# Splitting the PSUM ring, moving tables and casts, and halving the last chunk in a state-space and windowed-attention kernel

## The chip, the cores and the metric

The kernel runs on one core of one Trainium2 chip. The metric is the device time of one execution in microseconds (us), median of several. A profiled execution of each kernel gives the trace; its span is about 2 us shorter than its time. In tables and text, PE is TensorE's matmuls, DVE is VectorE, ACT is ScalarE, POOL is GpSimd and SP is the engine that issues most transfers. PSUM is the memory into which TensorE's matmuls write in these kernels, and SBUF is the one that holds tables and inputs; a *ring* is a pool of equal buffers that are taken in turn.

## The reference, cut to what matters

Four layers, each with a residual: a state-space convolution, a windowed attention, the same convolution again with the same parameters, and the attention again. The input has 2048 positions and 512 channels, in bf16.

```python
def _A_ref(u, A_re, A_im, B_re, B_im, C_re, C_im, log_dt, Dskip):
    ...
    P = jnp.exp(logdA[:, :, None] * l[None, None, :])           # 512 x 128 x 2048 powers
    K = jnp.einsum("dn,dnl,dn->dl", Cc, P, dB).real             # kernel: 512 x 2048
    ...                                                         # y = irfft(rfft(u) * rfft(K)) + u * Dskip
def _B_ref(x, wqkv, wo):      # H = 32 heads of 16, window W = 8, dilation 2
    ...
x = x + _A_ref(_layernorm(x), ...)      # first convolution: makes K too
x = x + _B_ref(_layernorm(x), ...)      # attention 1
x = x + _A_ref(_layernorm(x), ...)      # second convolution: K's spectra are reused
x = x + _B_ref(_layernorm(x), ...)      # attention 2
```

## The kernel before

The kernel `K` is not made by 2048 powers. A *ladder* squares the complex multipliers, VectorE builds two small *tables* of powers (`Xtab`, `Ytab`/`Y2tab`) per half chunk of 64 channels by repeated doubling, and TensorE contracts them (`psk`). There are eight such tables.

The convolution works on four chunks of 128 channels. `s1` is the first FFT stage (matmuls with a constant, copied out as `Z`). `s2` transposes `Z` (copied out as `zt`) and does the second stage; the spectra are `xc` for the input and `Kt` for the kernel. `finish` multiplies them (`pa`, `pb`, on VectorE), does the inverse of the second stage (`VT`) and the output stage, which adds the residual into `X`.

```python
def s2(self, Z, dst, what):
    for ch in range(2):
        pt = self.pst([128, 2, 2, 4, 128], BF)          # same PSUM ring as everything else
        ...                                             # 16 transposes
        zt = self.w.tile([128, 2, 2, 512], BF, name="zt", tag="zt")
        self.evac("zt", ...)                            # one copy of 128x2048
        for c2 in range(2):
            xp = self.pst([128, 2, 512])
            ...                                         # four matmuls
            self.evac(what, dst[:, ch * 2 + c2, :, :], xp[:])

def kernel_and_first_conv(...):
    ...
    ladder(nc, pp, pst, identf, raw, MA, MB, cb, nu, fill)
    # the ladder's SBUF is given back here; the tables are laid in it afterwards
    psum = es.enter_context(tc.tile_pool(name="k_ps", bufs=4, space=PSUM))
    T = Tables(nc, tc, es, MA, MB, cb, nu, psum, kscr)  # psk comes from the ring too
    cv = Conv(nc, tc, es, C, X, psum, ())               # every copy on ScalarE
    ...
    for dc in range(4):
        ...                                             # two tables, u_fft(dc), k_fft(dc-1), finish(dc-1)
    Kt = k_fft(3)
    cv.finish(3, xcs.pop(3), Kt)

def a_layer(...):                                       # second convolution
    ...
    for g in range(NG):
        ln_stats_group(...)                             # statistics, with TensorE idle
    for dc in range(4):
        xc = cv.u_fft(dc, rstd, nb, "dve")
        cv.finish(dc, xc, Kts[dc])
```

Of the kernel before, what the change touches and what calls it, by code (L numbers as in the profile page):

```python
# [72 lines left out]
def make_consts(nc, const, C):  # L73
    fc = _fft_consts()
    bones_np = np.zeros((128, 8), dtype=np.float32)
    for f in range(128):
        bones_np[f, f // 16] = 1.0
    for name in ("F1", "F1T"):
        C[name + "_h"] = nc.inline_tensor(_bf(fc[name]), name="c_" + name)
    todo = [("ident", _bf(np.eye(128)), BF), ("C2", _bf(fc["C2"]), BF), ("IC", _bf(fc["IC"]), BF),  # L80
            ("bones", _bf(bones_np), BF), ("onesr", _bf(np.ones((1, 128))), BF)]
    for i, (name, arr, dt) in enumerate(todo):
        h = nc.inline_tensor(arr, name="c_" + name)
        t = const.tile(list(arr.shape), dt, name="sb_" + name)
        (nc.sync if i % 2 == 0 else nc.scalar).dma_start(t[:], h.ap())
        C[name] = t


def load_f1(nc, pool, C):
    for name, eng in (("F1", nc.sync), ("F1T", nc.scalar)):  # L90
# [4 lines left out]
def load_x(nc, const, x2d):  # L95
    xv = x2d.rearrange("(p j) d -> p j d", j=NJ)
    X = const.tile([128, NJ, D], BF, name="X")
    for g in range(NG):
        (nc.sync if g % 2 == 0 else nc.scalar).dma_start(X[:, g * 4:(g + 1) * 4, :], xv[:, g * 4:(g + 1) * 4, :])
# [30 lines left out]
def ln_stats_group(nc, small, Xt, rstd, nb):  # L130
    stats = small.tile([128, 4, 6], F32, name="ln_stats", tag="ln_stats")
    mv = small.tile([128, 4, 2], F32, name="ln_mv", tag="ln_mv")
    for jj in range(4):
        nc.vector.bn_stats(stats[:, jj, :], Xt[:, jj, :])  # L134
    for jj in range(4):
        nc.vector.bn_aggr(mv[:, jj, :], stats[:, jj, :])
    mvb = small.tile([128, 4, 2], BF, name="ln_mvb", tag="ln_mvb")
    nc.vector.tensor_copy(mvb[:], mv[:])
    veps = small.tile([128, 4], BF, name="ln_veps", tag="ln_veps")
    nc.vector.tensor_scalar(veps[:], mvb[:, :, 1], EPS, None, ALU.add)  # L140
    den = small.tile([128, 4], BF, name="ln_den", tag="ln_den")
    nc.scalar.activation(den[:], veps[:], ACT.Sqrt)
    nc.vector.reciprocal(rstd, den[:])
    nc.vector.scalar_tensor_tensor(nb, mvb[:, :, 0], -1.0, rstd, ALU.mult, ALU.mult)


def layer_norm_group(nc, small, Xt, out_ap):
    rstd = small.tile([128, 4], F32, name="ln_rstd", tag="ln_rstd")
    nb = small.tile([128, 4], F32, name="ln_nb", tag="ln_nb")
    ln_stats_group(nc, small, Xt, rstd[:], nb[:])  # L150
    for jj in range(4):
        nc.vector.tensor_scalar(out_ap[:, jj, :], Xt[:, jj, :], rstd[:, jj:jj + 1], nb[:, jj:jj + 1],
                                ALU.mult, ALU.add)


class Conv:


    def __init__(self, nc, tc, es, C, X, psum, on_dve, zbufs=2, pbufs=2):
        self.nc, self.C, self.X, self.ps, self.on_dve = nc, C, X, psum, on_dve  # L160
# [5 lines left out]
    def pst(self, shape, dt=F32):  # L166
        return self.ps.tile(shape, dt, name="ps", tag="ps")
# [7 lines left out]
    def s1(self, rhs_j, drow=None):  # L175
        nc, F1 = self.nc, self.C["F1"]
        Z = self.z.tile([128, 2, 16, 128], BF, name="Z", tag="Z")
        for jq in range(NJ // 4):
            ps = self.pst([128, 2, 16, 32])
            for jj in range(4):  # L180
                j = jq * 4 + jj
                for r in range(2):
                    dk = drow is not None and j == 0 and r == 0
                    o = ps[:, r, :, jj * 8:(jj + 1) * 8]
# [3 lines left out]
            self.evac("z", Z[:, :, :, jq * 32:(jq + 1) * 32], ps[:])  # L188
        return Z

    def s2(self, Z, dst, what):
        nc, ident, C2 = self.nc, self.C["ident"], self.C["C2"]
        for ch in range(2):
            pt = self.pst([128, 2, 2, 4, 128], BF)
            for c2 in range(2):
                for r in range(2):
                    for g in range(4):
                        nc.tensor.transpose(pt[:, c2, r, g, :], Z[:, r, (ch * 2 + c2) * 4 + g, :], ident[:])  # L198
            zt = self.w.tile([128, 2, 2, 512], BF, name="zt", tag="zt")
            self.evac("zt", zt[:].rearrange("q c r k -> q (c r k)"), pt[:].rearrange("q c r g k -> q (c r g k)"))  # L200
            for c2 in range(2):
                xp = self.pst([128, 2, 512])
                nc.tensor.matmul(xp[:, 0, :], C2[:, 0, :], zt[:, c2, 0, :], start=True, stop=False)  # L203
                nc.tensor.matmul(xp[:, 0, :], C2[:, 2, :], zt[:, c2, 1, :], start=False, stop=True)
                nc.tensor.matmul(xp[:, 1, :], C2[:, 1, :], zt[:, c2, 0, :], start=True, stop=False)  # L205
                nc.tensor.matmul(xp[:, 1, :], C2[:, 0, :], zt[:, c2, 1, :], start=False, stop=True)  # L206
                self.evac(what, dst[:, ch * 2 + c2, :, :], xp[:])

    def u_fft(self, dc, rstd, nb, norm_eng):
        nc = self.nc  # L210
        dsl = slice(dc * DCH, (dc + 1) * DCH)
        U = self.one.tile([128, NJ, DCH], BF, name="U", tag="U")
        for j in range(NJ):
            if norm_eng == "act":
                nc.scalar.activation(U[:, j, :], self.X[:, j, dsl], ACT.Identity, bias=nb[:, j:j + 1],
                                     scale=rstd[:, j:j + 1])
            else:
                nc.vector.tensor_scalar(U[:, j, :], self.X[:, j, dsl], rstd[:, j:j + 1], nb[:, j:j + 1],
                                        ALU.mult, ALU.add)
        Z = self.s1(lambda j: U[:, j, :])  # L220
        xc = self.one.tile([128, 4, 2, 512], BF, name="xc", tag="xc", bufs=2)
        self.s2(Z, xc, "xc")
        return xc

    def finish(self, dc, xc, Kt):
        nc, IC, F1T, X = self.nc, self.C["IC"], self.C["F1T"], self.X
        dsl = slice(dc * DCH, (dc + 1) * DCH)
        VT = self.one.tile([128, 2, NJ, DCH], BF, name="VT", tag="VT")

        def inverse(c, pa, pb):  # L230
# [8 lines left out]
            for gh in range(2):  # L239
                self.evac("vt%d" % gh,  # L240
                          VT[:, :, :, c * 32 + gh * 16:c * 32 + gh * 16 + 16].rearrange("k r j x -> k (r j) x"),
# [3 lines left out]
        for c in range(5):  # L245
            cur = None
            if c < 4:
# [8 lines left out]
        for jh in range(2):  # L256
            ps = self.pst([128, 2, 4, DCH])
            for q in range(2):
                j0 = jh * 8 + q * 4
                nc.tensor.matmul(ps[:, q, :, :], self.C["ident"][:], X[:, j0:j0 + 4, dsl], start=True, stop=False,  # L260
                                 skip_group_check=True)
                for jj in range(4):
                    for r in range(2):
                        nc.tensor.matmul(ps[:, q, jj, :], F1T[:, j0 + jj, r, :], VT[:, r, j0 + jj, :],
                                         start=False, stop=(jj == 3 and r == 1), skip_group_check=True)
            nc.scalar.copy(X[:, jh * 8:(jh + 1) * 8, dsl], ps[:].rearrange("p q j d -> p (q j) d"))


def load_params(nc, pp, prm):
    raw = {}  # L270
    engs = [nc.sync, nc.scalar]
# [4 lines left out]
    for idx, name in enumerate(("A_im", "A_re", "C_re", "B_re", "C_im", "B_im")):  # L276
        t = pp.tile([128, 4, NM], BF, name="raw_" + name)
        engs[(idx + 1) % 2].dma_start(t[:], prm[name].rearrange("(t p) n -> p t n", p=128))
# [4 lines left out]
def ladder(nc, pp, pst, identf, raw, MA, MB, cb, nu, fill):  # L283
# [4 lines left out]
    nc.vector.tensor_copy(dtf[:], dtb[:])  # L288
    dt_bc = dtf[:].unsqueeze(2).to_broadcast([128, 4, NM])
# [4 lines left out]
    nc.vector.tensor_tensor(tb[:], raw["A_im"][:], dt_bc, ALU.mult)  # L294
    a = tmp("a_arg")
    nc.vector.tensor_tensor(a[:], raw["A_re"][:], dt_bc, ALU.mult)
    e = tmp("e_mag")
    nc.scalar.activation(e[:], a[:], ACT.Exp)
    nc.vector.tensor_scalar(tb[:], tb[:], 1.0 / TWO_PI, None, ALU.mult)
# [3 lines left out]
    nc.vector.tensor_tensor(ws[:], tb[:], rnd[:], ALU.subtract)  # L303
    sn = tmp("sn")
    nc.scalar.activation(sn[:], ws[:], ACT.Sin, scale=TWO_PI)
    tq = tmp("tq")
    rnd2 = tmp("rnd2")
    wc = tmp("wc")
    nc.vector.tensor_scalar(tq[:], tb[:], 0.25, None, ALU.add)
    nc.vector.tensor_scalar(rnd2[:], tq[:], MAGIC, MAGIC, ALU.add, ALU.subtract)  # L310
    nc.vector.tensor_tensor(wc[:], tq[:], rnd2[:], ALU.subtract)
    cs = tmp("cs")
    nc.scalar.activation(cs[:], wc[:], ACT.Sin, scale=TWO_PI)
    quad = pp.tile([128, 4, 4, NM], F32, name="quad")
    nc.vector.tensor_tensor(quad[:, :, 1, :], e[:], sn[:], ALU.mult)
    nc.vector.tensor_tensor(quad[:, :, 0, :], e[:], cs[:], ALU.mult)
# [30 lines left out]
    def multipliers(i, cur):  # L347
# [8 lines left out]
        nc.vector.tensor_scalar(MB[:, i, :, 0, :], src[:, 1], -1.0 if conj else 1.0, None, ALU.mult)  # L356
        nc.vector.tensor_scalar(MB[:, i, :, 1, :], src[:, 1], 1.0 if conj else -1.0, None, ALU.mult)
# [29 lines left out]
class Tables:  # L387
# [59 lines left out]
    def contract(self, X, Y, Y2, hc):  # L447

        nc = self.nc
        psk = self.ps.tile([128, 16, EY], F32, name="psk", tag="ps")  # L450
# [20 lines left out]
def kernel_and_first_conv(nc, tc, C, prm, X, raw_pool, kt_dram, kscr):  # L471
    with ExitStack() as es:
# [5 lines left out]
        rstd = mt.tile([128, NJ], F32, name="rstd")  # L478
        nb = mt.tile([128, NJ], F32, name="nb")
        small = es.enter_context(tc.tile_pool(name="k_small", bufs=2))  # L480
        with tc.tile_pool(name="k_prep", bufs=1) as pp, tc.tile_pool(name="k_pst", bufs=2, space=PSUM) as pst:
            raw = load_params(nc, pp, prm)
            identf = pp.tile([128, 128], F32, name="identf")
            nc.scalar.dma_start(identf[:], nc.inline_tensor(np.eye(128, dtype=np.float32), name="c_identf").ap())
            X = load_x(nc, raw_pool, X)
            make_consts(nc, raw_pool, C)
            load_f1(nc, mt, C)
# [3 lines left out]
            def fill(i):  # L491
                if 1 <= i <= 4:
                    g = i - 1
                    ln_stats_group(nc, small, X[:, g * 4:(g + 1) * 4, :], rstd[:, g * 4:(g + 1) * 4],
                                   nb[:, g * 4:(g + 1) * 4])
# [312 lines left out]
```

## Time and profile before

Median 750.1 us (749.71 to 750.54). The span of the profiled run is 746.9 us. Its stages, with borders read from the trace at the first and last instruction of a kind:

| border | us |
|---|---|
| first contraction (first `psk` matmul) | 75.4 |
| last table finished (last `Y2tab`) | 268.2 |
| last output of the first convolution (`X`) | 309.7 |
| attention 1: first transpose (`pt_x`) | 321.2 |
| second convolution: first `s1` matmul | 483.4 |
| its last `X` | 586.4 |
| attention 2: first transpose | 591.4 |
| end | 746.9 |

The next fence shows busy time by stretch of the kernel before: the stretch in us, its length, busy us and instructions of PE, PEld (weight loads), DVE, ACT and POOL, then the mean granted TensorE clock (1.00 is full), the DMA share and GB/s.

```profile
0.00:75.40 75.40, 18.68 (x95) 11.16 (x96) 64.00 (x149) 57.23 (x83) 0.60 (x8) 0.98 0.21 72
75.40:268.20 192.80, 118.03 (x2570) 85.83 (x2580) 151.91 (x268) 106.75 (x129) 1.69 (x12) 0.77 0.11 37
268.20:309.70 41.50, 26.04 (x432) 19.49 (x432) 6.22 (x10) 18.87 (x21) 0.96 (x1) 0.75 0.10 39
309.70:321.20 11.50, 0.00 (x0) 0.00 (x0) 9.23 (x24) 0.20 (x1) 5.10 (x1) 0.61 0.62 183
483.40:586.40 103.00, 79.22 (x716) 59.82 (x720) 56.24 (x126) 48.74 (x58) 0.00 (x0) 0.87 0.05 20
```

No engine is full over the whole span, but VectorE dominates the first two stretches (64 of 75 us, then 152 of 193), and TensorE dominates the second convolution (79 of 103). So in each stage the question is what the dominant engine waits for. The waits of VectorE between 100 and 270 us (engine and tile that waited, the releaser, us in total, times, longest):

```profile
DVE Ytab L433 <- PE psk L461: 21.5, 3, 7.2
DVE pa L250 <- ACT Kt L173: 15.4, 6, 6.9
```

At every other table VectorE stands up to 7.2 us until the contraction has finished reading an older one, and then for the kernel's spectrum. The waits of TensorE in the second convolution (484 to 591 us):

```profile
PE ps L203 <- DVE zt L171: 10.6, 8, 1.4
PE ps L198 <- ACT Z L173: 8.7, 4, 2.5
PE ps L264 <- DVE VT L171: 2.5, 4, 1.0
```

TensorE loses 2.7 us a chunk before the second-stage matmuls, because they wait for the transposed copy `zt`, and 2.2 us before the transposes, because they wait for `Z`. These three waits, 21.8 us, are nearly all of the 23.8 us in which PE is idle there.

### The profile page before, as it was taken

To read this page: it belongs to the slowest core of one execution; us is meant where nothing else is said; L and a number is where in the kernel's file an instruction comes from. 1 tells how busy PE (TensorE), PEld (TensorE's weight loads), DVE (VectorE), ACT (ScalarE), POOL (GpSimd) and SP (SyncE) were. 2 spreads that over 40 slices of the span, in tenths; PEclk is the share of its full clock that TensorE was granted. 3 is DMA by queue.
4 is the path that set the end of the run, shared out by engine and by line. 5 is a ranking of instruction groups with operands and counts; after the bars stand their busy time and mean duration, and the time that the engine had idled before them with its cause. 6 is when DMAs were issued, how large, how long until landed. Compare 5 with 4: busy or idle time off the path is not lost.

```text
span 746.9 us, 13529 instructions
## 1 busy us (share of the span) xinstructions
PE 479.3 (64%) x5863; PEld 304.3 (41%) x5908; DVE 506.0 (68%) x936; ACT 363.3 (49%) x436; POOL 8.4 (1%) x21
## 2 busy tenths in 40 slices
PE   0215166756756747459971889376787589934996
PEld 0212144543643534444551344155665445631443
DVE  4999996598598531482698983775544724998870
ACT  2998058468556526346433144344544365512434
POOL 0000000000000000300000000000000000000000
PEclk9999656887887885859985899779998789955999
DMA  8000000210200200500030000710000000030011
GB/s 288 0 0 1 29 31 1 86 31 1 86 31 1 86 31 1 169 1 0 2 101 0 1 0 1 279 59 1 2 1 1 0 1 1 2 99 0 1 57 56
DMA packets 14682, 28.75 MB, mean 38 GB/s; under 512 B 4769, under 2 KB 10274, under 8 KB 12834
## 3 DMA queue, kind: packets, MB, share of 16 engines
q1 hardware_dynamic: 10640, 20.26, 8.1%
q10 hardware_dynamic: 3984, 7.64, 2.8%
q8 instruction: 46, 0.75, 0.4%
q14 instruction: 12, 0.10, 0.0%
HBM read 15.86 MB, written 8.39 MB: 32 GB/s over the span
## 4 chain that ended last, share of the span: by engine, by line
PE 45%; DVE 29%; ACT 15%; issue 8%; DMA 3%; ACTq 0%; DVEq 0%
PE ps_qk L599 8%; PE po L710 5%; PE ps_o L727 4%; ACT Z L173 4%; PE ps_v L612 4%; ACT zt L173 4%; PE ps L198 3%; DVE ln_stats L134 3%; PE ps L203 2%; DVE Ytab L442 2%; DVE prodpv L704 2%; PE ps L205 2%; PE ps L206 2%; PE Lp L642 2%; DVE Y2tab L444 2%
## 5 line engine op out<-in xcount | busy, mean ns | idle before, releaser
L710 PE MATMUL po<-prodpv,sb_ident 128*128 128x512 bf16 x248 | 67.0, 402 | 35.0 <-DVE prodpv L696 31.3
L599 PE MATMUL ps_qk<-xnT,wqk 128*128 128x512 bf16 x248 | 59.7, 392 | 8.3 <-ACT xnT L586 7.4
L134 DVE BATCH_NORM_STATS2 ln_stats<-X 128x6 f32<-128x512 bf16 x64 | 43.0, 709 | 30.5 <-PE ps_o L727 12.3
L250 DVE TENSOR_TENSOR pa<-xc,Kt 128x1024 bf16<-128x1024 bf16 x32 | 22.0, 689 | 53.4 <-ACT Kt L173 38.5
L173 ACT CAST Z<-ps 128x1024 bf16<-128x1024 f32 x48 | 45.8, 1025 | 25.0 <-PE ps L185 25.0
L198 PE MATMUL ps<-sb_ident,Z 128*128 128x128 bf16 x384 | 35.4, 265 | 33.4 <-ACT Z L173 33.4
L710 PEld LDWEIGHTS <-sb_ident 128*128 128x128 bf16 x256 | 26.1, 102 | 67.1 <-issue 45.7
L696 DVE TENSOR_TENSOR prodpv<-V,Lsb 128x2048 bf16<-128x2048 bf16 (+1 forms) x40 | 42.2, 1115 | 16.3 <-PE po L710 16.0
L203 PE MATMUL ps<-zt,sb_C_99 128*128 128x512 bf16 x48 | 25.2, 525 | 43.0 <-ACT zt L173 32.4
L173 ACT CAST xc<-ps 128x1024 bf16<-128x1024 f32 x32 | 31.9, 1013 | 41.7 <-PE ps L206 41.7
L198 PEld LDWEIGHTS <-Z 128*128 128x128 bf16 x384 | 32.0, 123 | 42.0 <-ACT Z L173 35.9
L642 PE MATMUL Lp<-sb_bones,prodqk 128*128 128x8 bf16 x1024 | 34.5, 167 | 12.7 <-DVE prodqk L638 7.2
L173 ACT CAST VT<-ps 128x512 bf16<-128x512 f32 x48 | 26.5, 587 | 30.5 <-PE ps L238 30.5
L599 PEld LDWEIGHTS <-wqk 128*128 128x128 bf16 x256 | 25.6, 100 | 38.5 <-issue 11.8
L642 PEld LDWEIGHTS <-prodqk 128*128 128x128 bf16 x1024 | 32.2, 98 | 21.8 <-DVE prodqk L638 8.7
L458 PE MATMUL psk<-Ytab,Xtab 128*32 128x64 bf16 x1024 | 22.6, 208 | 26.7 <-DVE Ytab L442 18.0
L727 PE MATMUL ps_o<-wo_t,oT 128*128 128x512 bf16 x124 | 32.3, 379 | 6.7 <-ACT o L713 4.3
L236 PE MATMUL ps<-sb_IC,pb 128*128 128x256 bf16 x128 | 35.2, 275 | 1.0 <-DVE pb L251 1.0
L235 PE MATMUL ps<-sb_IC,pa 128*128 128x256 bf16 x128 | 35.3, 276 | 0.7 <-DVE pa L250 0.7
L237 PE MATMUL ps<-sb_IC,pb 128*128 128x256 bf16 x128 | 35.1, 274 | 0.0
L238 PE MATMUL ps<-sb_IC,pa 128*128 128x256 bf16 x128 | 35.0, 274 | 0.0
L173 ACT COPY zt<-ps 128x2048 bf16<-128x2048 bf16 x16 | 29.8, 1865 | 7.6 <-PE ps L198 7.4
(176 smaller groups left out, 1134.0 us busy)
## 6 DMA issues: line engine op xcount, KB each, us to landing
kt_scratch<-Kt SPq DMA_DIRECT2D x4, 1024.0 KB, 4.1
Vp<-V SPq DMA_DIRECT2D x2, 1568.0 KB, 9.6
sb_F1T<-c_F1T ACTq DMA_DIRECT2D x2, 1024.0 KB, 6.8
k_scratch<-KTq SPq DMA_DIRECT2D x8, 256.0 KB, 2.0
KT<-k_scratch SPq DMA_DIRECT2D x8, 256.0 KB, 2.8
Kt<-kt_scratch SPq DMA_DIRECT2D x2, 1024.0 KB, 14.6
Kt<-kt_scratch ACTq DMA_DIRECT2D x2, 1024.0 KB, 17.0
X<-in_A_u_dram ACTq DMA_DIRECT2D x2, 512.0 KB
```

The source lines that it names most:

```text
L134: nc.vector.bn_stats(stats[:, jj, :], Xt[:, jj, :])
L173: self.nc.scalar.copy(dst, src)
L198: nc.tensor.transpose(pt[:, c2, r, g, :], Z[:, r, (ch * 2 + c2) * 4 + g, :], ident[:])
L203: nc.tensor.matmul(xp[:, 0, :], C2[:, 0, :], zt[:, c2, 0, :], start=True, stop=False)
L235: nc.tensor.matmul(o, pa[:, 0, sl], IC[:, 0, :], start=True, stop=False)
L236: nc.tensor.matmul(o, pb[:, 1, sl], IC[:, 1, :], start=False, stop=False)
L237: nc.tensor.matmul(o, pb[:, 0, sl], IC[:, 2, :], start=False, stop=False)
L599: nc.tensor.matmul(ps[:, sc * 512:(sc + 1) * 512], wqk[:, ct, which * 512 + ft * 128: which * 512 + (ft + 1) * 128], xnT[:, ct, s0:s0 + 51 ...
L642: nc.tensor.matmul(Lp[f2][:, w, jj, :], pr[:, f2, jj * 128:(jj + 1) * 128], bones[:], start=True, stop=True)
L696: nc.vector.tensor_tensor(p2[:, ja - j0: ja - j0 + n, :].rearrange("p j (t d h) -> p (j t) d h", t=4, d=DH), V[:, ja - sh: ja - sh + n, :] ...
L710: nc.tensor.matmul(po[jj // 2][:, jj % 2, :], ident[:], p2[:, jj, :], start=(w == 0), stop=(w == W - 1))
L727: nc.tensor.matmul(ps[:, jj, :], oT[:, ft, j * 128:(j + 1) * 128], wo_t[:, ft, :], start=(ft == 0), stop=False)
```

## The change

The intent: give contraction, spectra and transposes PSUM buffers of their own; lay the tables where the ladder's memory isn't, so that they can begin before it is finished; take the casts of the multipliers off VectorE; and do the last chunk of the first convolution in two halves. The diff does more: it moves the layer norm statistics into the stage before, moves the first convolution's 64 normalizations and its input `zt` copies from ScalarE to VectorE, makes every `zt` copy half as large, gives `VT` a second buffer in the second convolution, and issues the second convolution's next transform ahead of this chunk's inverse. Cut to its core:

```diff
@@ ladder
-        nc.vector.tensor_scalar(MB[:, i, :, 0, :], src[:, 1], -1.0 if conj else 1.0, None, ALU.mult)
+        nc.scalar.activation(MB[:, i, :, 0, :], src[:, 1], ACT.Copy, scale=-1.0 if conj else 1.0)
         ...                                                    # and MB[..., 1, :]
@@ kernel_and_first_conv
+        psk = es.enter_context(tc.tile_pool(name="k_psk", bufs=1, space=PSUM))
+        T = Tables(nc, tc, es, MA, MB, cb, nu, psk, kscr)      # before the ladder's pools
         with tc.tile_pool(name="k_prep", bufs=1) as pp, ...:
             ...
-        psum = es.enter_context(tc.tile_pool(name="k_ps", bufs=4, space=PSUM))
-        T = Tables(nc, tc, es, MA, MB, cb, nu, psum, kscr)
-        cv = Conv(nc, tc, es, C, X, psum, ())
+        psT = es.enter_context(tc.tile_pool(name="k_psT", bufs=2, space=PSUM))
+        psA = es.enter_context(tc.tile_pool(name="k_psA", bufs=2, space=PSUM))
+        cv = Conv(nc, tc, es, C, X, psA, psT, ("zt_xc",))      # the input's zt on VectorE
         ...
-        Kt = k_fft(3)
-        cv.finish(3, xcs.pop(3), Kt)
+        ln_b.gather(X, 0, 0, NJ)                               # statistics of three chunks of X
+        xc = xcs.pop(3)
+        for h in range(2):
+            Kt = k_fft(3, h, h + 1)
+            cv.finish(3, xc, Kt, h * 2, h * 2 + 2)
+        ln_b.gather(X, 1, 0, NJ)
+        ln_b.finish(0, NJ)
@@ u_fft
-            if norm_eng == "act":
-                nc.scalar.activation(U[:, j, :], self.X[:, j, dsl], ACT.Identity, bias=..., scale=...)
-            else: ...
+            ln.norm(U[:, j, :], self.X[:, j, dsl], j)          # tensor_scalar on VectorE
@@ a_layer (second convolution)
+        xcs = {0: cv.u_fft(0, ln)}
         for dc in range(4):
-            xc = cv.u_fft(dc, rstd, nb, "dve")
-            cv.finish(dc, xc, Kts[dc])
+            if dc < 3:
+                xcs[dc + 1] = cv.u_fft(dc + 1, ln)
+            cv.finish(dc, xcs.pop(dc), Kts[dc])
+            if dc == 2:
+                ln_b.gather(X, 0, 0, NJ)
+        ln_b.gather(X, 1, 0, NJ)
+        ln_b.finish(0, NJ)
@@ ... (load queues, one range reduction less in the ladder, product buffers of attention 4 -> 3)
```

## The prediction

> **What bounds the kernel now.** Stages, from the timeline: first convolution with kernel generation (0 to 309 us), attention (to 472), second convolution (to 586), attention. From busy time by stretch and the waits:
> - Prologue: ladder starts at 26.5 us, first table whole at 75.3; VectorE has 64 us of work there.
> - Generation (100 to 270): VectorE busy 128 of 170 us; it waits 21.5 us for the contraction (psk) and 15.4 for Kt. One ring of four serves all PSUM users, so it stands behind FFT evictions. The Trainium skill (Perfetto Trace Analysis, Optimization Strategy) names such consistent bubbles as a sign of too little PSUM; the trace agrees (7.2 us at each odd table).
> - Tail (273 to 309): a serial chain, VectorE idle 22.7 us, then 12 us of weights and layer norm before attention's first transpose at 321.2.
> - Second convolution: 25 us a chunk, PE busy 19 to 20, waiting for Z (8.7 us in all) and zt (10.6). Before it, 10.4 us of layer norm with PE idle.
>
> **What the change does, costed.**
> 1. Prologue: 22 multiplier casts (0.34 us of VectorE each) go to ScalarE, one range reduction goes, ScalarE issues three loads instead of nine. VectorE work falls by 9 us and starts at 4.5 us instead of 10: first table at about 63 us. ScalarE (2.9 us a level) ends near 50.
> 2. Generation: own PSUM for the contraction removes most of both waits, but 64 normalizations (0.23 us) and 16 half-size zt copies (0.63) come onto VectorE: 24 us. From 63: seven tables of 20.2, plus 13.7, 10.1, 14.4 for spectrum products, 4 of stalls: last table at 247 instead of 268. Gain of 1 and 2 together: 21.
> 3. Tail: the order of instructions puts the halves one after the other on PE and ScalarE, and the weight reorder before the second half's products on VectorE: about 40 us instead of 37. Statistics and weights come earlier: attention starts 6 us after the last X instead of 11.5. Gain 2.
> 4. Attention: normalization no longer waits for statistics, 3 us each, twice. Three product buffers instead of four and statistics in the value stage lose 2.
> 5. Second convolution: statistics ride in the attention before: gain 7.5. The next chunk's transform ahead of this one's inverse, and finer zt: about 21.5 us a chunk, gain 14.
>
> Sum: 21 + 2 + 6 - 2 + 7.5 + 14 = 48.5. Predicted 702 us, range 684 to 722. Chances: faster 0.95, same 0.04, slower 0.01.
>
> The 128x512 spectra matmul takes 0.63 us after a gap and 0.38 in a dense stretch. The Trainium skill (TensorE: Matmul & The Clock Gate, Part 1) says activity releases the throttle; fewer gaps should raise the clock in the second convolution above 0.87.
>
> **What shows it.** First contraction at 60 to 66 us; from there VectorE over 92% busy to the last table at 243 to 253; its waits for psk and Kt under 8 us together; last table to attention's first transpose 50 to 53 us; attention's end to the next first-stage matmul about 3 us; chunk period of the second convolution 20 to 23 us; PE's wait for zt there under 5 us.
>
> **What would make it wrong.** VectorE, in program order, stalling for zt or U (a generation chunk over 54 us); PE waiting for PSUM with two wide buffers; a tail over 45 us; the second convolution staying at 25.

## The result, and the profile after

The changed kernel takes 695.25 us (693.33 to 697.3, 4 runs) against 750.14 us (4 runs) of the kernel before on the same chip. The ratio is 0.9269, 95% interval 0.9241 to 0.9296. Ratios here are the mean time of one kernel's fast runs over that of the other's of the same rounds, so not quite the ratio of the quoted medians. It is faster, inside the predicted range and 7 us below its centre.

The same view for the kernel after, by its own stage borders:

```profile
0.00:61.90 61.90, 5.51 (x22) 3.40 (x22) 54.74 (x117) 41.73 (x60) 0.61 (x8) 1.00 0.26 87
61.90:238.30 176.40, 123.74 (x2652) 90.76 (x2661) 168.69 (x346) 90.11 (x105) 1.51 (x12) 0.87 0.11 41
238.30:279.90 41.60, 26.04 (x498) 18.93 (x496) 15.65 (x34) 20.51 (x30) 6.06 (x1) 0.84 0.28 90
279.90:285.40 5.50, 0.02 (x1) 0.03 (x2) 4.98 (x36) 0.21 (x1) 0.00 (x0) 0.68 0.00 0
435.10:536.10 101.00, 79.55 (x716) 59.53 (x720) 62.67 (x149) 48.15 (x56) 0.00 (x0) 0.90 0.08 31
```

Set against the fence of before, line by line: the prologue is 13.5 us shorter; the table stage is 16.4 us shorter although VectorE does 16.8 us more work in it (it is now busy 168.69 of 176.40 us, 95.6%); the tail has the same length; the gap before attention is halved; and the second convolution, where the largest single gain of a later stage was expected, is 2 us shorter. All stages, from the two traces:

| stage | before, us | after, us | change | predicted |
|---|---|---|---|---|
| to first contraction | 75.4 | 61.9 | -13.5 | about -12 |
| first contraction to last table | 192.8 | 176.4 | -16.4 | about -9 |
| last table to last `X` | 41.5 | 41.6 | +0.1 | about +3 |
| last `X` to attention 1 | 11.5 | 5.5 | -6.0 | about -5 |
| attention 1, to its last `X` | 151.8 | 146.6 | -5.2 | -2 |
| layer norm before the second convolution | 10.4 | 3.1 | -7.3 | -7.5 |
| second convolution | 103.0 | 101.0 | -2.0 | -14 |
| last `X` to attention 2 | 5.0 | 5.1 | +0.1 | 0 |
| attention 2 | 155.5 | 150.2 | -5.3 | -2 |
| sum | 746.9 | 691.4 | -55.5 | -48.5 |

The first two rows were predicted as one term, 21; the split follows from the 63 us that the prediction gave for the first table. The next two were one term too (gain 2), and the attention's 6 less 2 is put half on each.

The waits of VectorE after, 60 to 260 us:

```profile
DVE pa L262 <- ACT Kt L180: 5.9, 1, 5.9
DVE zt L178 <- PE pt L208: 5.0, 7, 1.3
```

The wait for `psk`, 21.5 us before, is gone. The one wait for `Kt` is that of the last chunk, after the last table. And the waits of TensorE in the second convolution, 438 to 535 us:

```profile
PE pt L208 <- ACT Z L180: 7.7, 4, 2.1
PE psA L276 <- DVE VT L178: 5.5, 4, 1.4
PE psA L247 <- DVE pa L262: 4.0, 1, 4.0
PE psA L219 <- DVE zt L178: 0.9, 2, 0.7
```

This is where the expected 14 us went. The wait for `zt` did fall as predicted, from 10.6 to 0.9 us. But the wait for `VT` rose from 2.5 to 5.5, a new wait of 4.0 for `pa` appeared, and the one for `Z` stayed. So 9.7 us were gained on one wait, and 7.0 lost on one that grew and one that is new. What VectorE does in the last chunk shows one of them (VectorE's instructions in order: start, us, what, count, and the idle time before it):

```profile
515.15 0.68 DVE L178 CAST VT<-psA 128x512 bf16<-128x512 f32 x1
518.24 7.46 DVE L146 BATCH_NORM_STATS2 ln_st_b<-X 128x6 f32<-128x384 bf16 x16 [2.40 <-ACT X L278]
525.61 1.27 DVE L178 CAST VT<-psA 128x512 bf16<-128x512 f32 x2
526.80 0.68 DVE L262 TENSOR_TENSOR pa<-xc,Kt 128x1024 bf16<-128x1024 bf16 x1
```

Sixteen statistics for the next layer norm stand in VectorE's queue before the last chunk's copies. VectorE runs its queue in order, so the copies wait behind 7.46 us of work that nothing needs yet. The Trainium skill (PSUM — Partial Sum Buffer, section Engine vs sequencer instructions) says that these queues are strict FIFO; this trace agrees. In the steady chunks a smaller form of the same thing happens: the products of chunk c+1 stand before the copy of chunk c. When `X` is written out by ScalarE shows the period:

```profile
470.28 2.12 ACT L278 CAST X<-psA 128x1024 bf16<-128x1024 f32 x2 [2.79 <-PE psA L276]
493.67 2.12 ACT L278 CAST X<-psA 128x1024 bf16<-128x1024 f32 x2 [2.72 <-PE psA L276]
517.19 2.12 ACT L278 CAST X<-psA 128x1024 bf16<-128x1024 f32 x2 [2.72 <-PE psA L276]
```

A chunk takes 23.4 us, with PE busy for some 19 of them.

### The profile page after: what moved, and what is told of

It reads as the page before. It is cut to its first block, busy times and chain, and to the rows that moved or that the text cites. A ratio compares the mean times of both kernels' runs of the same rounds, so it can differ in the third digit from the quotient of the medians.

```text
span 691.4 us, 13674 instructions
## 1 busy us (share of the span) xinstructions
PE 465.4 (67%) x5930; PEld 297.7 (43%) x5977; DVE 512.5 (74%) x984; ACT 331.3 (48%) x388; POOL 8.2 (1%) x21
## 5 line engine op out<-in xcount | busy, mean ns | idle before, releaser
L193 PE MATMUL psA<-U,sb_F_128 128*128 128x128 bf16 x256 | 24.1, 242 | 47.5 <-issue 38.5
L180 ACT CAST Z<-psA 128x1024 bf16<-128x1024 f32 (+1 forms) x52 | 46.4, 960 | 20.1 <-issue 17.3
L180 ACT CAST xc<-psA 128x1024 bf16<-128x1024 f32 x32 | 32.0, 1012 | 44.6 <-PE psA L222 37.4
L193 PEld LDWEIGHTS <-sb_F_128 128*128 128x128 bf16 x416 | 27.1, 104 | 57.9 <-issue 50.7
L208 PE MATMUL pt<-sb_ident,Z 128*128 128x128 bf16 x384 | 38.4, 268 | 19.5 <-ACT Z L180 19.5
L180 ACT CAST VT<-psA 128x512 bf16<-128x512 f32 x48 | 26.6, 588 | 44.4 <-PE psA L250 44.4
L660 PE MATMUL Lp<-sb_bones,prodqk 128*128 128x8 bf16 x1024 | 35.3, 167 | 14.7 <-DVE prodqk L656 9.4
L247 PE MATMUL psA<-sb_IC,pa 128*128 128x256 bf16 x128 | 36.2, 283 | 9.6 <-DVE pa L262 9.6
L159 DVE TENSOR_SCALAR U<-X,ln_rstd_a,ln_nb_a 128x128 bf16<-128x128 bf16 x128 | 33.5, 307 | 7.2 <-PE psA L193 7.2
L178 DVE COPY zt<-pt 128x1024 bf16<-128x1024 bf16 x32 | 21.8, 688 | 20.6 <-PE pt L208 20.5
L248 PE MATMUL psA<-sb_IC,pb 128*128 128x256 bf16 x128 | 36.2, 283 | 1.1 <-DVE pb L263 1.1
L249 PE MATMUL psA<-sb_IC,pb 128*128 128x256 bf16 x128 | 36.0, 281 | 0.0
L250 PE MATMUL psA<-sb_IC,pa 128*128 128x256 bf16 x128 | 35.9, 281 | 0.0
```

Source lines behind the costliest of these rows:

```text
L180: self.nc.scalar.copy(dst, src)
L193: nc.tensor.matmul(o, F1[:, j, r, :], rhs_j(j), start=True, stop=not dk)
L208: nc.tensor.transpose(pt[:, r, g, :], Z[:, r, i * 4 + g, :], ident[:])
L247: nc.tensor.matmul(o, pa[:, 0, sl], IC[:, 0, :], start=True, stop=False)
L248: nc.tensor.matmul(o, pb[:, 1, sl], IC[:, 1, :], start=False, stop=False)
L249: nc.tensor.matmul(o, pb[:, 0, sl], IC[:, 2, :], start=False, stop=False)
```

## The experiments

Twelve kernels ran, all with correct results, all over three rounds beside runs of the kernel before, whose medians were 750.7 to 751.9 us. Stage borders come from each run's trace. "After" is the changed kernel with its 695.25 us; each edit is made on it. The kernel after ran in other rounds than these, beside runs of the kernel before of 750.1 us, so the last column is good to a few us only; where it is small, the intervals of the ratios decide (0.9241 to 0.9296 for after).

| run | what differs from after | median, us | ratio to before (95%) | against after |
|---|---|---|---|---|
| psk_shared | contraction back in the spectra's ring | 701.93 | 0.9361 (0.9336 to 0.9387) | +6.7 |
| casts_dve | multiplier casts back on VectorE | 701.56 | 0.9349 (0.9327 to 0.9370) | +6.3 |
| tables_late | tables laid after the ladder's memory is free | 698.05 | 0.9294 (0.9266 to 0.9322) | +2.8 |
| norm_act | first convolution's normalizations back on ScalarE | 684.54 | 0.9118 (0.9093 to 0.9143) | -10.7 |
| gather_late | statistics after the second convolution | 690.56 | 0.9195 (0.9168 to 0.9223) | -4.7 |
| a2_inter | second convolution interleaved by stage | 680.50 | 0.9060 (0.9031 to 0.9089) | -14.7 |
| a2_seq | second convolution in the order of before | 693.05 | 0.9218 (0.9180 to 0.9256) | -2.2 |
| wv_pool | value-weight reorder on GpSimd | 690.82 | 0.9188 (0.9142 to 0.9233) | -4.4 |
| whole_last | last chunk in one piece | 690.22 | 0.9192 (0.9165 to 0.9218) | -5.0 |
| best1 | norm_act, a2_inter, gather_late, wv_pool | 659.42 | 0.8768 (0.8740 to 0.8796) | -35.8 |
| best2 | best1, `zt` on ScalarE, halves interleaved | 651.22 | 0.8673 (0.8644 to 0.8702) | -44.0 |
| best4 | best1, `zt` on ScalarE, last chunk whole | 649.11 | 0.8640 (0.8614 to 0.8666) | -46.1 |

### The named parts of the change, undone one at a time

**psk_shared.** The contraction takes its PSUM from one ring of three with the spectra; the transposes keep their own pool.

```diff
-        psk = es.enter_context(tc.tile_pool(name="k_psk", bufs=1, space=PSUM))
-        T = Tables(nc, tc, es, MA, MB, cb, nu, psk, kscr)
+        psA = es.enter_context(tc.tile_pool(name="k_psA", bufs=3, space=PSUM))
+        T = Tables(nc, tc, es, MA, MB, cb, nu, psA, kscr)
```

> The changed kernel, with the contraction back in one PSUM ring with the first stages, spectra and inverses (three wide buffers; the transposes keep their own pool). Theory: the contraction again stands behind the FFT in the ring, VectorE waits about 7 us for it at every odd table and for Kt as before; the last table comes at about 252 us instead of 238 and the total is about 709, 14 over the changed kernel. Rival: what was gained came from the finer zt copies and the shorter prologue; then the ring costs under 4 us (695 to 699).

It lost 6.7 us, between the two theories. First contraction at 71.7 us instead of 61.9, last table at 247.7 instead of 238.3. VectorE's waits between 45 and 260 us, and the table stage as a view by stretch:

```profile
DVE pa L262 <- ACT Kt L180: 8.3, 6, 4.8
DVE Ytab L442 <- PE psk L470: 4.9, 2, 4.6
```

```profile
71.70:247.70 176.00, 112.23 (x2590) 83.03 (x2600) 161.00 (x317) 85.10 (x100) 1.60 (x12) 0.84 0.12 41
```

The wait for `psk` came back with 4.9 us, not with the 21.5 of before. The later first contraction is no loss by itself: in this run it comes after the first chunk's transform, and VectorE has been idle for 7.2 us until then, as in the kernel after. VectorE loses its time afterwards: up to the last table it is idle for 15.0 of 176.0 us, against 7.7 of 176.4, and waits for `psk` (4.9) and `Kt` (3.5 of the 8.3; the rest comes later) are there. So the separate pool is worth its 6.7 us. The repeated bubble of before went for another reason as well. What that is wasn't isolated: the transposes keep their own pool in this run, and VectorE's extra 17 us of work bring it to each table later. Both are only argued.

**casts_dve.** The two `MB` casts per level are `nc.vector.tensor_scalar` again.

> The changed kernel, with the 22 multiplier casts back on VectorE. Theory: VectorE's work bounds the prologue, so 22 x 0.34 = 7.5 us come back, the first contraction starts at about 69 us instead of 61.9 and the total is about 702. Rival: ScalarE's chain of 2.9 us a level bounds the ladder; then taking the casts off it ends the ladder 10 us sooner and the total is 693 to 697.

701.56 us, first contraction at 70.3 us, last table at 245.1. The cost theory predicted 702 and 69, and holds: VectorE is the bound of the prologue, and in this run ScalarE waits for it there (6.7 us for the ladder's `lad`, in four places). So moving the casts gains 6.3 us.

**tables_late.** The one line that lays the tables (`T = Tables(...)`) moves back to behind the ladder.

> The changed kernel, with the memory of the tables taken after the ladder's is given back, as it was before the change. Theory: no table step may run before the ladder's last reader, ScalarE's last cast at 50.1 us; in the changed kernel about 7 us of table work on VectorE run before that, so the first contraction starts at about 69 us and the total is about 702. Rival: VectorE's work is the same in sum and only its order changes; then the total rises under 2 us.

+2.8 us by the medians, between the theories; the interval of the ratio overlaps that of after, so a difference in the total is not shown. The first contraction is 9.8 us later (71.7 us), but the last table only 5.4 us (243.7): while the tables can't start, the scheduler puts the first chunk's normalizations, from 39.1 us, into the time that VectorE would have idled. The placement lets work start earlier, but much of the 9.8 us is only reordered.

**whole_last.** The last chunk in one piece.

```diff
-        for h in range(2):
-            Kt = k_fft(3, h, h + 1)
-            cv.finish(3, xc, Kt, h * 2, h * 2 + 2)
+        Kt = k_fft(3)
+        cv.finish(3, xc, Kt)
```

> Edit: the last chunk of the first convolution is transformed and multiplied in one piece again, as in the kernel before; all else is as in the changed kernel. Theory A (the halves are made one after the other, each with a shorter chain, so their gain and their extra evictions cancel: the stretch from last table to last output was 41.5 us before and 41.6 after the change): total within 2 us of 695. Theory B (halves do shorten the tail and something else, such as the 4 us wait for the value weights, ate it): total 697 to 700 us. Theory C (halves cost): 690 to 693.

690.22 us: 5.0 us **faster** without the halves, the theory that they cost. Last table to last `X` takes 35.8 us (239.1 to 274.9), against 41.6 with halves and 41.5 in the kernel before. So the rest of the change shortened the tail by 5.7 us, and the halves as they stand here gave it back. They are emitted one after the other, and the second half's multiplier products also stand behind the reorder of the attention's value weights (kernel after, VectorE):

```profile
259.60 0.48 DVE L125 MEMSET Vp<- 128x512 uint32 x1 [5.48 <-PE psA L195]
267.91 2.19 DVE L119 COPY wv<-wvn 128x512 bf16<-128x512 bf16 x4 [7.82 <-DMA wvn<-in_B_wqkv_dram]
270.02 0.69 DVE L262 TENSOR_TENSOR pa<-xc,Kt 128x1024 bf16<-128x1024 bf16 x1
```

VectorE waits 7.82 us for the weights' transfer, copies for 2.19, and only then makes `pa`, although its `Kt` was ready at about 266 us. The next run tells how much of the halves' cost that is.

**wv_pool.** That reorder goes to GpSimd.

```diff
-            nc.vector.tensor_copy(wv[:, :, ft * 128 ...
+            nc.gpsimd.tensor_copy(wv[:, :, ft * 128 ...
```

> Edit: the reorder copies of the late value weights are made on GpSimd instead of VectorE. Theory A (after the last table VectorE stands 4 us at a copy that waits for its weight transfer, while the multiplier product behind it is ready and the last inverse waits for it): the last chunk's product starts 3 to 4 us earlier, total 691 to 692 us. Theory B (the copies lie beside the path or the slower engine makes the value projection late): total within 2 us of 695, or slower.

690.82 us, the theory that the copies stood in the way. The second half's product now waits for nothing but `Kt`:

```profile
268.11 0.69 DVE L262 TENSOR_TENSOR pa<-xc,Kt 128x1024 bf16<-128x1024 bf16 x1 [6.00 <-ACT Kt L180]
```

Last table to last `X` takes 36.3 us (240.3 to 276.6) with the halves kept, only 0.5 more than in one piece (35.8). In one piece the reorder is hardly in the way: its copies are done at 259.8 us, and the first `Kt` at 259.3. So by these two traces most of what whole_last gained was the wait behind the weights, and the halves by themselves cost little. Attention 1 begins at 282.2 instead of 285.4 us. The median gains 4.4 us, and its interval is the widest of all runs (0.9142 to 0.9233), so the trace's 3 us is the safer number. The four copies take 1.1 to 1.6 us each on GpSimd, from 269.6 us, and nobody needs them before attention's value projection at 317.9. One product that VectorE makes beside them takes 1.60 us instead of 0.68; why was not followed up.

### The riders of the change

**norm_act.** The 64 normalizations of the first convolution return to ScalarE; those of the second stay on VectorE.

```diff
-            ln.norm(U[:, j, :], self.X[:, j, dsl], j)
+            if act:
+                self.nc.scalar.activation(U[:, j, :], self.X[:, j, dsl], ACT.Identity, bias=..., scale=...)
+            else:
+                ln.norm(U[:, j, :], self.X[:, j, dsl], j)
```

> The changed kernel, with the 64 normalizations of the first convolution back on ScalarE (0.40 us each there, 0.23 on VectorE). Theory: the generation is bound by VectorE's work (169 of 176 us busy), so taking 14 us from it brings the last table 10 to 14 us sooner: total about 683. Rival: [...]the 6.4 us a chunk stand before evictions that VectorE and PE need, so waits for Kt and zt come back and the total stays within 4 us of 695.

684.54 us, 10.7 faster than after. The table stage is VectorE's, so work that ScalarE has time for does not belong there. The Trainium skill says so (Perfetto Trace Analysis, section Optimizing Scalar/DVE Operations: if VectorE "is saturated, offloading some work to Scalar (or even GPSIMD) may make sense"), and this run agrees: VectorE was busy for 95.6% of that stage. The run above is another case, for there VectorE stood idle at a transfer.

The run also tells why the table stage came out shorter than the sum of its work. The stage shrank by 7.0 us (61.7 to 231.3: 169.6 us, against 176.4 from 61.9), not by the 14.7 us that 64 normalizations of 0.23 us would be:

```profile
61.70:231.30 169.60, 121.05 (x2641) 86.49 (x2652) 159.85 (x285) 106.46 (x150) 1.42 (x12) 0.87 0.12 42
```

The timeline of norm_act in a doubling step, `tb` and then the sum that reads it:

```profile
67.03 0.68 DVE L425 TENSOR_TENSOR tb<-Xtab,MB 128x1024 bf16<-128x1024 bf16 x1
67.75 0.69 DVE L426 TENSOR_TENSOR Xtab<-ta,tb 128x1024 bf16<-128x1024 bf16 x1
68.36 0.23 DVE L446 COPY Ytab<-cb 128x128 bf16<-128x128 bf16 x1
```

And the same step in the kernel after, with a normalization in between:

```profile
92.84 0.68 DVE L421 TENSOR_TENSOR tb<-Xtab,MB 128x1024 bf16<-128x1024 bf16 x1
93.45 0.31 DVE L159 TENSOR_SCALAR U<-X,ln_rstd_a,ln_nb_a 128x128 bf16<-128x128 bf16 x1
93.67 0.68 DVE L422 TENSOR_TENSOR Xtab<-ta,tb 128x1024 bf16<-128x1024 bf16 x1
```

The sum, which needs the result of the instruction just before it, starts 0.72 us after it; an instruction that doesn't need it starts 0.61 us after (67.75 to 68.36, or 92.84 to 93.45). So a dependent pair loses 0.11 us, and a normalization between the two costs 93.67 - 92.84 - 0.72 = 0.11 us instead of its 0.22 (93.45 to 93.67). These are no single cases: in norm_act's trace 26 sums of this size start 0.71 to 0.72 us after their `tb`, and 31 instructions `tb`, which do not need the `ta` before them, 0.59 to 0.62 us after it. In the kernel after, 49 of the 64 normalizations stand alone between two such table steps, 13 stand in one row and fill one gap, and 2 stand beside a `zt` copy. From these counts the estimate is 49 x 0.11 + (13 x 0.22 - 0.11) + 2 x 0.22 = 8.6 us, against 7.0 measured; so the gaps explain most of the difference from 14.7, not all of it.

**a2_seq.** The second convolution in the order of before: transform and inverse of a chunk, then the next chunk.

> Edit: in the second convolution alone the transform of the next chunk is no longer emitted ahead of this chunk's inverse, as in the kernel before. Theory A (emitting it ahead does remove the wait for the zt copies, some 10 us, but gives it back as waits for VT copies behind the next chunk's products and for the last chunk's statistics): total within 3 us of 695 either way, the waits for zt copies back at about 10 us, those for VT copies down to 2 to 3. Theory B (of the prediction: the transform ahead is worth 10 to 14 us there): total 705 to 709 us.

693.05 us, within 3 us of after and, by its median, 2.2 faster. The stage takes 97.6 us (436.9 to 534.5) instead of 101.0. TensorE's three largest waits there:

```profile
PE pt L208 <- ACT Z L180: 7.7, 4, 2.1
PE psA L276 <- DVE VT L178: 3.9, 4, 1.0
PE psA L219 <- DVE zt L178: 3.8, 5, 2.2
```

So issuing the whole transform ahead, which the prediction gave most of its 14 us, gains nothing. The theory behind that was half wrong: the wait for `zt` came back with 3.8 us, not 10. Most of it was removed by what this run keeps of the change, in whatever order: copies of half the size, their own PSUM, a second buffer for `VT`. The wait for `VT` fell from 5.5 to 3.9 only, so 1.6 of its 3.0 us of growth go with the transform ahead. The 4.0 us for `pa` are gone although the statistics are emitted where they were: it takes both, the statistics in that place and the transform ahead. The same page of the Trainium skill (Perfetto Trace Analysis, section Optimizing Scalar/DVE Operations) says that breaking up instructions may let work be completed sooner where VectorE is not saturated but causes bubbles elsewhere; this run fits that (10.6 us before, 3.8 here, in the same order), but does not isolate the size of the copies.

**gather_late.** The 16 statistics of 7.46 us are emitted after the convolution.

```diff
-            if dc == 2:
-                ln_b.gather(X, 0, 0, NJ)
+        ln_b.gather(X, 0, 0, NJ)
         ln_b.gather(X, 1, 0, NJ)
```

> Edit: the statistics of the second normalization's first part, which the changed kernel puts into VectorE's queue ahead of the second convolution's last transform copies, are emitted after that convolution. Theory A (part of the missing gain of the second convolution is the last chunk: 16 statistics, 7.46 us, stand ahead of the copies that TensorE and ScalarE wait for): the last chunk goes from about 18.9 us to 12 to 14 us, the 4.0 us wait of the last inverse for the multiplier product is gone, total about 690 us (689 to 692); the statistics then cost up to 2 us after the convolution. Theory B (the statistics only fill idle time and something else holds the last chunk): total within 2 us of 695.

690.56 us, 4.7 faster, as the first theory has it. The stage falls to 97.1 us (436.7 to 533.8) and the 4.0 us wait for `pa` is gone from TensorE's list. Attention 2 starts 5.1 us after the last `X`, just as in the kernel after, so the later statistics cost nothing there.

**a2_inter.** The stages of two chunks are interleaved, so that TensorE has matmuls to do while the copies that it will need next are made.

```diff
         for dc in range(4):
-            if dc < 3:
-                xcs[dc + 1] = cv.u_fft(dc + 1, ln)
-            cv.finish(dc, xcs.pop(dc), Kts[dc])
+            Z = cv.u_s1(dc + 1, ln) if dc < 3 else None      # first stage of the next chunk
+            VT = cv.fin_inv(dc, xcs.pop(dc), Kts[dc])        # inverse of this one, while Z is copied
+            if dc < 3:
+                xcs[dc + 1] = cv.u_s2(Z)                     # second stage of the next, while VT is copied
+            cv.fin_out(dc, VT)
```

> Edit: in the second convolution the next chunk's first stage runs before this chunk's inverse, and its second stage between the inverse and the output stage, so that TensorE has matmuls to do while the copies that it waits for are made. Theory A (the steady period of 23.4 us is TensorE's 19.1 us of work plus waits for the Z and VT copies, a matter of order): the period falls to 19.5 to 21 us, the Z waits of 7.7 us fall below 2, total 684 to 689 us. Theory B (the period is set by ScalarE's and VectorE's evictions, not by the order): the period stays at 23 us and the total within 2 us of 695.

680.50 us, 14.7 faster than after: what the prediction had put on this stage, got by another order of the same instructions, and 3.5 us better than the best of the expected range. The stage takes 87.7 us (435.5 to 523.2). TensorE's waits from 438 to 523 us, and ScalarE's writes of `X`:

```profile
PE psA L253 <- DVE pa L268: 3.8, 1, 3.8
PE psA L219 <- DVE zt L178: 2.3, 6, 0.5
PE pt L208 <- ACT Z L180: 1.2, 1, 1.2
PE psA L288 <- DVE VT L178: 1.0, 1, 1.0
```

```profile
465.82 1.01 ACT L290 CAST X<-psA 128x1024 bf16<-128x1024 f32 x1 [0.31 <-PE psA L288]
484.93 1.01 ACT L290 CAST X<-psA 128x1024 bf16<-128x1024 f32 x1 [0.31 <-PE psA L288]
504.04 1.01 ACT L290 CAST X<-psA 128x1024 bf16<-128x1024 f32 x1 [0.31 <-PE psA L288]
```

The waits for `Z` and `VT` in these lists, 13.2 us after, are 2.2 us here (14.1 and 4.0 with the smaller lines for `Z` that both lists leave out), and a steady chunk takes 19.1 us. TensorE is busy for 17.4 of them, at a granted clock of 1.00; in the kernel after it is 19.1 of 23.4 at 0.93. Of the 13.3 us that the stage gained, 9.2 are idle time of TensorE and 4.1 shorter busy time for the same 716 matmuls. The largest wait that is left is the 3.8 us behind the statistics, once.

### A version that beats both

**best1** puts four edits together: norm_act, wv_pool, a2_inter and gather_late.

> Edit: four edits at once on the changed kernel: the first convolution's normalizations on ScalarE, the value-weight reorder on GpSimd, the second convolution interleaved (next chunk's stages between this chunk's inverse and output), the statistics of its last chunk after it. If the gains lie in different stages and add (10.7 of the normalizations, 14.7 of the interleaving, 3 to 4 of the weights, 2 to 4 of the statistics beyond the interleaving): 662 to 667 us. If they overlap (the later stage takes back what the earlier gained): 670 to 678 us.

659.42 us, better than the range for gains that add, so nothing was given back between these stages.

**best2** adds two edits: the 16 `zt` copies of the input in the first convolution go to ScalarE, and the halves of the last chunk are interleaved.

```diff
-        cv = Conv(nc, tc, es, C, X, psA, psT, ("zt_xc",))
+        cv = Conv(nc, tc, es, C, X, psA, psT, ())
...
+        k_s2(k_s1(0), 0)
+        Z1 = k_s1(1)
+        VT0 = cv.fin_inv(3, xc, Kt, 0, 2)
+        k_s2(Z1, 1)
+        cv.fin_out(3, VT0, 0, 2)
+        cv.finish(3, xc, Kt, 2, 4)
```

> Edit: as the four edits at once, and in addition the first convolution's 16 remaining transposed copies on ScalarE and the last chunk's halves interleaved (second half's first stage before the first half's inverse). Theory A (the table stage is still bound by VectorE, 160 of 170 us, so 11 us less work there shortens it by 7 to 10 us, and the interleaved halves take 2 to 4 us off the tail): 650 to 657 us. Theory B (ScalarE, then with some 120 us of work there and each copy 1.02 us in place of 0.69, delays the transforms and thereby the products; or PE is the next limit with 121 us): no gain or up to 5 us worse than the four edits.

651.22 us, a gain of 8.2. The last table ends at 214.8 instead of 230.1 us: 15.3 us less, about the copies' 10.9 us on VectorE and the 3.0 us that it waited for their transposes in best1. But the tail, from there to the last `X`, grew from 33.3 to 40.6 us, so half of it was given back.

**best4** tells whether the halves did that: as best2, with the last chunk whole.

> Edit: as the kernel of 651.2 us (five edits and interleaved halves), but with the last chunk of the first convolution in one piece. Theory A (halves cost by themselves, in whatever order, as the run that undid them alone gained about 5 us): 646 to 649 us, the stretch from last table to last output 36 to 38 us instead of 40.6. Theory B (interleaving had already removed their cost, and the 40.6 us are the work of the chunk before, which VectorE's shorter table stage no longer hides): 650 to 653 us.

649.11 us. The intervals of the two ratios overlap, and the tail is 40.0 us (215.8 to 255.8) against 40.6. The total lies between the ranges of the two theories; the tail decides for the second. So the halves cost nothing measurable any more, which the moved reorder alone may explain (wv_pool, 36.3 against 35.8 us); that the interleaving did it is not shown. The longer tail fits the second theory too: VectorE now finishes its tables before TensorE and ScalarE have finished the chunk before. TensorE works 31.4 of these 40.0 us, and 23.7 of 33.3 in best1. best4 is the fastest kernel, 13.6% under the kernel before.

## Why the prediction was right or wrong

The total was right (702 predicted, 695.25 measured). But four terms were mis-sized, and that the sum came so close is in part luck, because their errors offset each other: 8.9 us too little for the prologue and table stage, 6.5 too little for the attentions, 3.9 too little for tail and gap, 12 too much for the second convolution.

- **First contraction at 60 to 66 us.** Right: 61.9. The two mechanisms were tested by undoing them: casts 6.3 us; placement of the tables 9.8 us at this border, though its 2.8 us in the total are not clear of noise.
- **VectorE over 92% busy in the table stage, under 8 us of waits for `psk` and `Kt`.** Right: 95.6%, and 0 and 5.9 us. Separate PSUM for the contraction is worth 6.7 us by itself; it does not explain the whole vanished bubble.
- **Last table at 243 to 253 us.** Wrong, it was 238.3. The term that failed is "64 normalizations (0.23 us) and 16 half-size zt copies (0.63) ... 24 us". The normalizations' share of 14.7 us measured 7.0, mostly because they fill the 0.11 us that dependent table steps leave open. The prediction added durations where part of them fits into gaps.
- **Tail about 40 us, 3 more than before.** The stretch from last table to last `X` stayed at 41.6 (41.5 before). Of its two reasons, the weight reorder before the second half's products is shown: moving it shortens the tail to 36.3 us. The halves' own cost is then about 0.5 us (35.8 in one piece). The 5.0 us of whole_last and the 3 to 4 of wv_pool are largely the same time and do not add. What was missed is that the rest of the change shortens this tail by 5.7 us. The prediction's 50 to 53 us from last table to attention came out as 47.1.
- **Layer norm gap about 3 us.** Right: 3.1 instead of 10.4.
- **Attentions: gain 3 each, loss 1 each.** The loss was right; the gain was forecast at half its size. From the first transpose to the first logits matmul, the same 188 matmuls take 34.0 us instead of 40.1, as the next two fences show (kernel before, then after; attention 2 does the same, 33.9 instead of 39.9). The logits part takes 1.1 us longer (36.4 instead of 35.3), and the rest is as long as before.

```profile
321.20:361.30 40.10, 35.90 (x188) 18.88 (x193) 16.51 (x52) 23.08 (x26) 0.00 (x0) 0.86 0.00 1
```

```profile
285.40:319.40 34.00, 32.96 (x188) 17.32 (x193) 8.40 (x20) 22.60 (x23) 0.00 (x0) 0.95 0.00 0
```

TensorE's idle time falls from 4.2 to 1.0 us (40.10 - 35.90, 34.00 - 32.96): these are the 3 us that the prediction named. The trace names ScalarE's `xnT` copies as what TensorE waited for (3.7 us before, 0.8 after); that the normalization, group by group, paced these copies is the prediction's reason, and no run tests it. The other 2.9 us are TensorE's busy time for the same instructions, at a granted clock of 0.95 instead of 0.86; the prediction had applied that reading to the second convolution alone. The Trainium skill (TensorE: Matmul & The Clock Gate, Part 1) says that activity releases the throttle; the trace agrees (0.95 with 1.0 us of pauses, 0.86 with 4.2).

- **Second convolution: "about 21.5 us a chunk, gain 14".** This is the step that failed: 23.4 us a chunk and a gain of 2.0. Its reason, a wait for `zt` that disappears, happened (10.6 to 0.9 us). But 14 us are more than that wait ever was, so part of the wait for `Z` had to go as well, and it stayed (8.7 before, 7.7 and 0.9 in two places after): issuing the transform ahead put no other matmuls in front of the transposes that wait for `Z`. And the prediction took the removed wait as gained time and did not ask what stands in VectorE's queue after it: the next chunk's products ahead of this chunk's `VT` copy (+3.0 us, of which a2_seq gives back 1.6), and the statistics ahead of the last chunk's copies (+4.0 us for `pa`). gather_late, a2_seq and a2_inter show it from three sides: without the statistics there, 97.1 us; without the transform ahead, 97.6; with TensorE's stages interleaved, 87.7.
- **Clock above 0.87 there.** Right, but little: 0.90 against 0.87. In best4, where TensorE is idle for 9.3 us there instead of 21.4, it is 0.98, and TensorE's busy time for the same matmuls is 71.9 us instead of 79.6.

The clock has a part in a2_inter's gain, as said there. Not tested on the chip by an edit: the earlier statistics (the gap before attention 1 and the layer norm gap), which by the two traces give 13.3 us, and the attentions' 10.5. For these the traces alone speak.

## What to carry to other kernels

A wait that a change removes is gained only if the engine's next wait was already over; read the queue of the engine that will have to deliver next, in the order in which the trace shows it, and look for work standing there that nobody needs yet. To pipeline across chunks, interleave single stages, so that each copy is hidden by another chunk's matmuls, and don't issue a whole stage sequence ahead. And once an engine is 95% busy, weigh every instruction moved onto it even if it seems to remove a wait: here, taking 64 small instructions and 16 copies off it again gave more than any named part of the change.

## What the Trainium skill lacked or had wrong

- *Perfetto Trace Analysis*, section Optimization Strategy, reads consistent bubbles as a possible lack of buffers. The case agrees in part only: with the contraction back in the spectra's PSUM ring, 4.9 of 21.5 us of the bubble returned (and 6.7 us of time). What else made the gap was not isolated; that it also depends on when the waiting engine arrives is only argued.
- *VectorE: DVE Perf Modes*, section The DRAIN you can't avoid, says that waiting for each result costs copies nothing extra. That was measured on copies; for table steps of 128x1024 here, an instruction that reads the result just written starts 0.72 us after it, an independent one 0.61 us after. Its rules for kernel authors lack the consequence: an independent instruction put between two such steps costs 0.11 instead of 0.22 us, and taking 64 of them out of the stage shortened it by 7.0 us, not 14.7.
- *TensorE: Matmul & The Clock Gate*, Part 1, calls the idle state throttled. The granted clock in these profiles reads 1.00 over the first 61.9 us, in which TensorE works for 5.5 us, and 0.61 in an idle stretch of 11.5 us after work. So a clock read over an early idle stretch says nothing.
- No page was found that says in what order to issue the stages of successive chunks which share the same engines, as in this FFT convolution. The same matmuls took 101.0 us with the next transform ahead, 97.6 in sequence and 87.7 with stages interleaved.
